# Warm products that read the preamble's constant ones instead of zeros written by VectorE

## The chip, the cores and the metric

One core of one Trainium2 chip. The metric is the device time of one execution in microseconds (us), the median of several. "Span" is the time in the trace from the first to the last instruction; it is about 2.2 us less.

## The reference

Two branches on the same normalised input, added to it: a diagonal state-space layer (S5) and a gated MLP with a spatial product. 2048 rows of 640 columns, bf16 in and out.

```python
x = A_x                                              # (1, 2048, 640)
xn = _layernorm(x, axis=-1)
return x + _A_ref(xn, ...) + _B_ref(xn, ...)         # S5 scan; gelu, layernorm, spatial product, gate
# ... _A_ref, _B_ref and the input setup left out
z = _gelu(einsum('bsd,df->bsf', x, w_in))            # the first matmuls of _B_ref
```

## The kernel before

The kernel describes its work as a graph of operations with assumed durations, plans an order for every engine from them, and derives the semaphore waits from the bytes that each operation reads and writes. A change of an assumed duration can therefore move instructions far away.

The parts that the change touches, and two others:

```python
# loads in the order of the SyncE queue: x tiles and quarters of w_in
FIRST = "x0 x1 x2 h002 h024 h045 x3 h103 x4 h135 x5"
# ...
dve(lambda e: e.memset(zero_m.ap(512), 0.0), [], [zero_m.iv(0, 1024)], 0.25, "zero")
# ... GpSimd builds the identity
act(lambda e: e.activation(zero_m.ap(8, BF16, 1024), zero_m.ap(8), ACT.Gelu_apprx_tanh), [zero_m.iv(0, 1024)],
    [zero_m.iv(1024, 16)], 1.4, "gelu table", bias=9000)      # loads the table early
NW = 7
for n in range(NW):                                           # warms TensorE's clock
    pe(lambda e: e.matmul(ps[:, 7, :], zero_m.ap(128), zero_m.ap(512), start=True, stop=True),
       [zero_m.iv(0, 1024)], [bank(7)], 0.43, "warm")
# ...
DMA_T = tuple(range(7, 16))           # tiles 7 to 15 are transposed by DMA, 0 to 6 by TensorE
def xn_T(i, b=None):
    xn = xc_m[i] if i in EARLY else xns[i]
    if i in DMA_T:
        dma("sp", xnTv[:, :, i * 128:(i + 1) * 128], xn.ap(D), [xn.iv()], xnT_iv(i, i + 1), ..., transpose=True)
        return
    # ... else transposes on TensorE, then a copy out of PSUM by VectorE or ScalarE
```

Behind this come the matmuls of the second half of z (helpers at L701 and L722 in the trace), the scan's inputs, the first half of z, the spatial product and the output. From about 21 us on TensorE works almost without a gap. In the lines, ps is PSUM, the memory that this kernel's matmuls write; PEq is TensorE's sequencer.

Of the kernel before, what the change touches and what calls it, by code (L numbers as in the profile page):

```python
# [7 lines left out]
ACT = mybir.ActivationFunctionType  # L8
# [20 lines left out]
class _Graph:  # L29



    EPS0 = 0.12
    LOOSE, LOOSE_BY = ("cy", "P", "Q", "h7", "fix"), 0.8
    TEPS = 12.0
    DMA_LAT = 2.0
# [68 lines left out]
    def plan(self):  # L105
        ops = self.ops
        keep = dict((o, r) for r, o in self.keep)
        pe = [o for o in ops if o.eng == "pe"]
        nxt = {a: b for a, b in zip(pe, pe[1:])}
        for op in ops:  # L110
            op.start = -1.0
        for op in reversed(ops):
            t = 0.0
            for s in op.succs:
                t = max(t, s.tail)
            own = op.occ + op.lat
            if op.nbytes:
                own += op.nbytes / self.DMA_BW
            t += own
            n = nxt.get(op)  # L120
            if n is not None:
                t = max(t, n.tail + op.occ)
            op.tail = t + op.bias
        free = {}
        dma_free = 0.0
        order = {}
        for op in ops:
            op.npred = len(op.preds)
            op.rdy = 0.0
        avail = {}  # L130
        for op in ops:
            if op.npred == 0:
                avail.setdefault(op.eng, []).append(op)
        pei = 0
        left = len(ops)
        eps = 0.12
        while left:
            best = None
            for eng, lst in avail.items():
                if not lst:  # L140
                    continue
                f = free.get(eng, 0.0)
                if eng == "pe":
                    if pei >= len(pe) or pe[pei].npred:
                        continue
                    cand = pe[pei]
                    st = max(f, cand.rdy)
                else:
                    if eng == "act" and keep:
                        held = {}  # L150
                        for o in lst:
                            t = max(f, o.rdy)
                            if o not in keep:
                                for k, r in keep.items():
                                    if k.start < 0 and t < r + 0.05 and t + o.occ > r + self.KEEP_BY:
                                        t = r + k.occ
                                        break
                            held[o] = t
                        s0 = min(held.values())
                        lst2 = [o for o in lst if held[o] <= s0 + eps]  # L160
                        cand = max(lst2, key=lambda o: o.tail)
                        st = max(f, cand.rdy, s0 if cand not in keep else 0.0)
                        if best is None or st < best[0]:
                            best = (st, cand)
                        continue
                    s0 = min(max(f, o.rdy) for o in lst)
                    cand = max((o for o in lst if max(f, o.rdy) <= s0 + (self.EPS0 if s0 < self.TEPS else eps)), key=lambda o: o.tail)
                    st = max(f, cand.rdy)
                if best is None or st < best[0]:
                    best = (st, cand)  # L170
            st, op = best
            eng = op.eng
            avail[eng].remove(op)
            if eng == "pe":
                pei += 1
            op.start = st
            free[eng] = st + op.occ
            if op.nbytes:
                if op.lat > 2.2:
                    dma_free = max(st + 1.25, dma_free) + op.nbytes / 270e3  # L180
                    free[eng] = st + {163840: 1.28, 819200: 3.6}.get(op.nbytes, 1.45)
                    op.done = dma_free + 2.2
                else:
                    at = max(st + op.occ + 0.9, dma_free)
                    dma_free = at + op.nbytes / (self.DMA_BW0 if at < self.DMA_T0 else self.DMA_BW1 if at < self.DMA_T1 else self.DMA_BW)
                    op.done = dma_free + op.lat - 0.9
            else:
                op.done = st + op.occ + op.lat
            order.setdefault(eng, []).append(op)
            left -= 1  # L190
            for s in op.succs:
                s.npred -= 1
                at = op.start + op.occ if eng == "pe" == s.eng else op.done
                if eng != s.eng and s.eng in ("act", "dve") and s.name.startswith(self.LOOSE):
                    at += self.LOOSE_BY
                if at > s.rdy:
                    s.rdy = at
                if s.npred == 0:
                    avail.setdefault(s.eng, []).append(s)
        self.order = order  # L200
        self.end = max(o.done for o in ops)
        return order
# [38 lines left out]
D = 640  # L241
# [9 lines left out]
def bass_parallel_sum__ssm_conv_s5__mixer_gmlp__prompt_kernel(  # L251
# [17 lines left out]
    with _cl.ExitStack() as _stack, nc.Block() as block:  # L269
# [236 lines left out]
        def load_dskip(after):  # L506
# [6 lines left out]
        dma("act", dk_m.ap(128)[0:16, :], B_w_in[0:640:40, FH:FH + 128], [], [dk_m.iv()], 4096, "touch", bias=9500)  # L513


        dve(lambda e: e.memset(zero_m.ap(512), 0.0), [], [zero_m.iv(0, 1024)], 0.25, "zero")
        pool(lambda e: e.memset(ident_m.ap(128), 0.0), [], [ident_m.iv()], 0.25, "id0")
        pool(lambda e: e.affine_select(out=ident_m.ap(128), in_=ident_m.ap(128), compare_op=ALU.not_equal,
                                       fill=1.0, base=0, pattern=[[-1, 128]], channel_multiplier=1),
# [2 lines left out]
        C("e", 40)  # L522
        pool(lambda e: e.memset(C("half"), -0.5), [], [Civ("half")], 0.2, "mhalf")
        pool(lambda e: e.memset(C("e"), math.e), [], [Civ("e")], 0.2, "e")
        act(lambda e: e.activation(zero_m.ap(8, BF16, 1024), zero_m.ap(8), ACT.Gelu_apprx_tanh), [zero_m.iv(0, 1024)],
            [zero_m.iv(1024, 16)], 1.4, "gelu table", bias=9000)
        NW = 7
        for n in range(NW):
            pe(lambda e: e.matmul(ps[:, 7, :], zero_m.ap(128), zero_m.ap(512), start=True, stop=True),
               [zero_m.iv(0, 1024)], [bank(7)], 0.43, "warm")  # L530

        pslot = [0]

# [21 lines left out]
        ACT_Z2 = (8, 12)  # L555
        NHALF = 4
        SINS = 20
        XT_ACT = (6,)
        BT_AT, BT_DEP = 10, 11
        LASTN = 480  # L560
# [53 lines left out]
        def ln_x(i):  # L614
            xm = xs[i]
            x = xm.ap(D)
            mean, rstd = mrv[:, i, 0:1], mrv[:, i, 1:2]
            mi, ri = mr_m.iv(i * 8, 4), mr_m.iv(i * 8 + 4, 4)
            if i in ACT_LN:
                sq = xn_m[i]  # L620
                act(lambda e: e.activation(sq.ap(D), x, ACT.Copy, scale=1.0 / D, accum_out=mean),
                    [xm.iv()], [sq.iv(), mi], ca(D, acc=1), "lnsum%d" % i)
                act(lambda e: e.activation(sq.ap(D), x, ACT.Square, scale=D ** -0.5, accum_out=stv[:, i, 1:2]),
                    [xm.iv()], [sq.iv(), siv(i, 1, 2)], ca(D, acc=1), "lnsq%d" % i)
                dve(lambda e: e.scalar_tensor_tensor(stv[:, i, 13:14], mean, mean, stv[:, i, 1:2],
                                                     op0=ALU.mult, op1=ALU.subtract, reverse1=True),
                    [siv(i, 1, 2), mi], [siv(i, 13, 14)], 0.07, "lnv%d" % i)
            else:

                held = xnT_iv(2, 3) if i == 3 else [xns[i - 1].iv()] if i in HELD else []  # L630
                dve(lambda e: e.bn_stats(stv[:, i, 0:6], x[:, 0:320]), [xm.iv()] + held, [siv(i, 0, 6)], 0.41, "bn%da" % i)
                dve(lambda e: e.bn_stats(stv[:, i, 6:12], x[:, 320:640]), [xm.iv()] + held, [siv(i, 6, 12)], 0.41, "bn%db" % i)
                dve(lambda e: e.bn_aggr(stv[:, i, 12:14], stv[:, i, 0:12]), [siv(i, 0, 12)], [siv(i, 12, 14)], 0.13,  # L633
                    "bna%d" % i)
            (dve if i in LNE_DVE else pool)(
                lambda e: e.tensor_scalar(stv[:, i, 14:15], stv[:, i, 13:14], 1e-5, None, op0=ALU.add),
                [siv(i, 13, 14)], [siv(i, 14, 15)], 0.07 if i in LNE_DVE else 0.22, "lne%d" % i)
            pool(lambda e: e.tensor_tensor(rstd, stv[:, i, 14:15], C("half")[:, 0:1], ALU.pow),
                 [siv(i, 14, 15), Civ("half")], [ri], 0.55, "rstd%d" % i)
            xn = xn_m[i]  # L640
            xns[i] = xn
            mu = mean if i in ACT_LN else stv[:, i, 12:13]
            dve(lambda e: e.tensor_scalar(xn.ap(D), x, mu, rstd, op0=ALU.subtract, op1=ALU.mult),  # L643
                [xm.iv(), ri, mi if i in ACT_LN else siv(i, 12, 13)], [xn.iv()], cd(D, 4) + 2 * PTR, "xn%d" % i)

        def xn_T(i, b=None):
            xn = xc_m[i] if i in EARLY else xns[i]
# [892 lines left out]
```

## Time and profile before

| | before |
|---|---|
| median, lowest and highest of the first three executions | 261.84, 261.57, 261.86 us |
| span of the profiled execution | 259.4 us |
| TensorE busy | 255.2 us, 98% |
| VectorE busy | 244.3 us, 94% |
| first warm product, first transpose, first real matmul | 1.19, 4.32, 6.08 us |

In a line of the timeline the two first numbers are start and duration in us; what stands in brackets is the idle time of the engine before it and what ended that. In a list of waits the numbers are total us, times, longest. In the chain of waits they are start and duration of each piece.

### The profile page before, as it was taken

To read this page: it belongs to the slowest core of one execution; us is meant where nothing else is said; L and a number is where in the kernel's file an instruction comes from. 1 tells how busy PE (TensorE), PEld (TensorE's weight loads), DVE (VectorE), ACT (ScalarE), POOL (GpSimd) and SP (SyncE) were. 2 spreads that over 40 slices of the span, in tenths; PEclk is the share of its full clock that TensorE was granted. 3 is DMA by queue.
4 is the path that set the end of the run, shared out by engine and by line. 5 is a ranking of instruction groups with operands and counts; after the bars stand their busy time and mean duration, and the time that the engine had idled before them with its cause. 6 is when DMAs were issued, how large, how long until landed. Compare 5 with 4: busy or idle time off the path is not lost.

```text
span 259.4 us, 4334 instructions
## 1 busy us (share of the span) xinstructions
PE 255.2 (98%) x1496; PEld 152.4 (59%) x1500; DVE 244.3 (94%) x567; ACT 179.8 (69%) x323; POOL 26.3 (10%) x50
## 2 busy tenths in 40 slices
PE   7999999999999999999999999999999999999996
PEld 3554554444446777755555555555567777777774
DVE  4899999799999999999999999999999999999943
ACT  6899999799986545442333496873979987895110
POOL 3567065112000000000000000000000000000000
PEclk9999999999999999999999999999999999999999
DMA  6947699999506893399998969991242565457611
GB/s 199 312 121 114 130 175 215 216 299 238 73 1 126 202 207 136 111 316 182 246 217 182 248 159 196 225 209 52 56 133 73 141 172 132 103 140 217 161 63 54
DMA packets 90324, 42.49 MB, mean 164 GB/s; under 512 B 73054, under 2 KB 90302, under 8 KB 90302
## 3 DMA queue, kind: packets, MB, share of 16 engines
q1 hardware_dynamic: 89982, 42.09, 67.2%
q8 instruction: 12, 0.20, 0.3%
q10 hardware_dynamic: 320, 0.12, 0.2%
q14 instruction: 10, 0.08, 0.1%
HBM read 12.28 MB, written 12.45 MB: 95 GB/s over the span
## 4 chain that ended last, share of the span: by engine, by line
PE 95%; DMA 3%; SPq 0%; DVE 0%; issue 0%
PE ps L1116 32%; PE ps L1264 23%; PE ps L701 18%; PE ps L795 17%; PE ps L722 3%; DMA arena<-arena 2%; PE ps L1271 2%; DMA arena<-in_B_w_in_dram 2%; SPq L409 0%; PE ps L659 0%; DVE arena L675 0%; DVE arena L643 0%; DVE arena L1329 0%; DVE arena L633 0%
## 5 line engine op out<-in xcount | busy, mean ns | idle before, releaser
L1116 PE MATMUL ps<-arena 128*128 128x432 bf16 x448 | 81.9, 346 | 0.0
L1116 PEld LDWEIGHTS ps<-arena 128*128 128x128 bf16 x448 | 43.8, 98 | 37.9
L1264 PE MATMUL ps<-arena 128*128 128x320 bf16 (+2 forms) x456 | 64.5, 296 | 0.0
L1264 PEld LDWEIGHTS ps<-arena 128*128 128x128 bf16 x456 | 44.2, 98 | 17.1
L701 PE MATMUL ps<-arena 128*128 128x432 bf16 x280 | 51.9, 346 | 0.2 <-DMA arena<-arena 0.2
L901 ACT ACTIVATE arena<-arena 128x512 bf16<-128x512 bf16 x70 | 46.2, 714 | 1.3 <-DVE arena L905 1.3
L701 PEld LDWEIGHTS ps<-arena 128*128 128x128 bf16 x280 | 34.6, 124 | 16.5 <-DMA arena<-arena 0.6
L795 PE MATMUL ps<-arena 128*128 128x512 bf16 x196 | 43.0, 379 | 0.2
L1129 ACT ACTIVATE arena<-ps,arena 128x432 f32<-128x432 f32 (+1 forms) x32 | 19.8, 620 | 24.9 <-PE ps L1116 23.7
L795 PEld LDWEIGHTS ps<-arena 128*128 128x128 bf16 x200 | 19.6, 98 | 23.5
L824 DVE SCALAR_TENSOR_TENSOR arena<-arena 128x512 f32<-128x512 bf16 x35 | 25.7, 743 | 0.0
L800 ACT CAST arena<-ps 128x512 bf16<-128x512 f32 x40 | 22.1, 602 | 3.7 <-PE ps L795 3.7
L905 DVE TENSOR_TENSOR arena<-arena 128x1024 bf16<-128x1024 bf16 (+1 forms) x42 | 24.3, 593 | 0.0
L779 ACT ACTIVATE arena<-ps 128x864 bf16<-128x864 f32 x16 | 14.3, 891 | 13.9 <-PE ps L701 10.6
L1293 ACT COPY ps<-ps 128x320 f32<-128x320 f32 x24 | 9.9, 411 | 19.8 <-PE ps L1264 19.5
L1285 DVE TENSOR_TENSOR arena<-ps,arena 128x320 bf16<-128x320 f32 (+1 forms) x40 | 18.0, 482 | 5.3 <-PE ps L1271 3.6
L846 DVE TENSOR_TENSOR arena<-arena 128x512 f32<-128x512 f32 (+2 forms) x40 | 21.3, 548 | 0.0
L1071 DVE TENSOR_TENSOR arena<-arena 128x1024 bf16<-128x1024 bf16 x32 | 21.1, 682 | 0.1
L829 DVE SCALAR_TENSOR_TENSOR arena<-arena 128x256 bf16<-128x256 bf16 (+1 forms) x35 | 16.6, 475 | 0.0
L826 DVE SCALAR_TENSOR_TENSOR arena<-arena 128x256 bf16<-128x256 bf16 (+1 forms) x35 | 16.5, 474 | 0.0
L1231 DVE TENSOR_TENSOR arena<-arena 128x640 bf16<-128x640 bf16 x32 | 14.6, 482 | 0.0
L715 ACT ACTIVATE arena<-arena 128x864 bf16<-128x864 bf16 x12 | 11.1, 922 | 0.0
(118 smaller groups left out, 255.8 us busy)
## 6 DMA issues: line engine op xcount, KB each, us to landing
g_scratch<-arena SPq DMA_DIRECT2D x16, 224.0 KB, 2.7
z_scratch<-arena SPq DMA_DIRECT2D x16, 216.0 KB, 2.4
arena<-z_scratch SPq DMA_DIRECT2D x8, 432.0 KB, 4.2
arena<-in_A_x_dram SPq DMA_DIRECT2D x16, 160.0 KB, 3.6
base_scratch<-arena SPq DMA_DIRECT2D x16, 160.0 KB, 2.2
arena<-base_scratch SPq DMA_DIRECT2D x16, 160.0 KB, 3.0
out_dram<-arena SPq DMA_DIRECT2D x15, 160.0 KB, 2.7
arena<-in_B_w_in_dram SPq DMA_DIRECT2D x8, 216.0 KB, 4.2
```

The source lines that it names most:

```text
L701: r = e.matmul(ps[:, b + h, 0:FG], lhs(k), winv[:, k, hcol * FH + h * FG:hcol * FH + (h + 1) * FG], start=(k == 0), stop=(k == ND - 1))
L795: r = e.matmul(ps[:, b, :], btv[:, ri, k, q * 128:(q + 1) * 128], xnTv[:, k, tq * 512:(tq + 1) * 512], start=(k == 0), stop=(k == ND - 1))
L800: act(lambda e: e.copy(o[:, ri, tq], ps[:, b, :].rearrange("p (m j) -> p j m", j=8)), [bank(b)], [l_m.iv((q * 8 + j) * 1024 + ri * 512 + t ...
L824: dve(lambda e: e.scalar_tensor_tensor(tv, prev, lr, cur, op0=ALU.mult, op1=ALU.add), pr + [l_iv(q, j)] + cr, [t.iv()], cd(512) + PTR, nm ...
L846: tt = lambda o, a, b, op: (lambda e: e.tensor_tensor(o, a, b, op))
L901: act(lambda e, pv=pv, hv=hv, lo=lo, sc=sc: e.activation(pv, hv[:, lo:lo + 2, 1:257], ACT.Identity, scale=sc), [h.iv(), Civ(cn)], [m.iv((q ...
L905: dve(lambda e, mv=mv, lq=lq: e.tensor_tensor(lq, lq, mv, ALU.add), li + [m.iv(0, 1024 * n)], li, cd(512 * n, 2), "fix%s%d%d" % (nm, q0, j))
L1071: dve(lambda e: e.tensor_tensor(o.ap(1024), x.ap(1024), y.ap(1024), op), [x.iv(), y.iv()] + S_HELD.get(j, []), [o.iv()], cd(1024, 2), "%s_ ...
L1116: r = e.matmul(ps[:, bk, 0:FG], lv_[:, k, :], rv[k], start=(first and k == 0), stop=(k == 7), skip_group_check=True)
L1129: act(lambda e: e.activation(o, pb(bk), ACT.Identity, bias=bias), [bank(bk)] + bi, [dst], ca(FG, psum=True, ptr=1), name)
L1264: r = e.matmul(ps[:, bk, c0:c1], lf(q), rf(q)[:, c0:c1], start=(first and q == 0), stop=(q == 7), skip_group_check=True)
L1285: dve(lambda e: e.tensor_tensor(o[0][:, c0:c1], ps[:, bk, c0:c1], y[0][:, c0:c1], ALU.add), [bank(bk), y[1]], [o[1]], cd(c1 - c0), "%s_%d" ...
```

## The change

Its intent: the warm products need some operand, no matter which. The preamble of every program already writes constants, a bf16 one per partition among them. If the products read that with a step of zero, VectorE's memset and the wait for it go; the products start earlier, and there is room for an eighth.

```diff
-        dve(lambda e: e.memset(zero_m.ap(512), 0.0), [], [zero_m.iv(0, 1024)], 0.25, "zero")
+        ones = lambda n: nc.const_aps.tensor(1.0, (128, n), BF16)
...
-        act(lambda e: e.activation(zero_m.ap(8, BF16, 1024), zero_m.ap(8), ACT.Gelu_apprx_tanh), [zero_m.iv(0, 1024)],
-            [zero_m.iv(1024, 16)], 1.4, "gelu table", bias=9000)
-        NW = 7
+        act(lambda e: e.activation(zero_m.ap(8), ones(8), ACT.Gelu_apprx_tanh), [], [zero_m.iv(0, 16)], 1.4, "gelu table",
+            bias=9000)
+        NW = 8
         for n in range(NW):
-            pe(lambda e: e.matmul(ps[:, 7, :], zero_m.ap(128), zero_m.ap(512), start=True, stop=True),
-               [zero_m.iv(0, 1024)], [bank(7)], 0.43, "warm")
+            pe(lambda e: e.matmul(ps[:, 7, :], ones(128), ones(512), start=True, stop=True), [], [bank(7)], 0.427, "warm")
... (an empty table of additions to priorities, and a bias of 0.0: without effect)
```

## The prediction

> **What bounds the kernel now.** I read the page's busy table first, then the chain of work that ended last, then the waits of TensorE, and only then the first 22 us in order of time, because the change touches nothing later.
>
> Busy table and clock row of the page:
>
> ```profile
> span 259.4 us, 4334 instructions
> ...
> PE 255.2 (98%) x1496; PEld 152.4 (59%) x1500; DVE 244.3 (94%) x567; ACT 179.8 (69%) x323; POOL 26.3 (10%) x50
> ...
> PEclk9999999999999999999999999999999999999999
> ```
>
> TensorE works for 255.2 of 259.4 us. Those that are left, about 4.2 us, are all that a change without effect on the matmuls themselves could win. The granted clock is full in the row of 40 slices; as shown below, that row does not show the slow first microseconds.
>
> Waits of TensorE in the whole span, and then the chain of waits in its first 20 us:
>
> ```profile
> PE ps L529 <- DVE arena L516: 1.2, 1, 1.2
> PE ps L722 <- DMA arena<-in_B_w_in_dram: 0.3, 1, 0.3
> PE ps L701 <- DMA arena<-arena: 0.2, 1, 0.2
> ```
>
> ```profile
> 2.12 3.91 DMA arena<-in_B_w_in_dram
> 6.03 0.05 issue
> 6.08 1.44 PE ps L722 x6
> ...
> 15.35 0.29 PE ps L659 x5
> 15.64 0.02 issue
> 15.67 0.49 DVE arena L675
> 16.16 0.36 DVE arena L643
> 16.51 0.03 DVE arena L633
> 16.54 4.44 DMA arena<-arena
> ```
>
> TensorE waits three times only. The first wait, 1.2 us, is the one that the change aims at: the warm products (L529) wait for VectorE's zeros (L516). But the chain that sets the end does not go through it. It goes from the issues on the SyncE queue into the load of the weights w_in, which lands at 6.03, and the first real matmul (L722) starts at 6.08. From there TensorE has only 0.2 us of wait left. So the start of the kernel is bound by a transfer whose issues begin at 0.74, and what TensorE does ahead of 6.08 is worth nothing by itself.
>
> The first microseconds in order of time:
>
> ```profile
> 0.86 0.27 DVE L516 MEMSET arena<- 128x256 uint32 x1 [0.86 <-PEq L1525]
> 1.18 1.28 ACT L525 ACT_TABLE_LOAD   x1 [1.18 <-PEq L1525]
> 1.19 3.17 PE L529 MATMUL ps<-arena 128*128 128x512 bf16 x7 [1.19 <-DVE arena L516]
> ...
> 2.48 0.21 ACT L525 ACTIVATE arena<-arena 128x8 bf16<-128x8 bf16 x1
> 3.01 0.74 ACT L572 ACTIVATE arena<-arena 128x640 bf16<-128x640 bf16 x1 [0.32 <-DMA arena<-in_A_x_dram]
> 3.01 0.49 DVE L583 BATCH_NORM_STATS2 arena<-arena 128x6 f32<-128x320 bf16 x1 [1.88 <-DMA arena<-in_A_x_dram]
> ...
> 4.32 0.45 PEld L659 LDWEIGHTS ps<-arena 128*128 128x128 bf16 x5 [0.87 <-DVE arena L577]
> ```
>
> The reader should see that VectorE idles 1.88 us after the memset until x0 lands, that ScalarE idles 0.32 us after its table, and that the first transposes at 4.32 wait for VectorE's centred x0 (L577), not for the warm products.
>
> **What the Trainium skill says.** First, "TensorE: Matmul & The Clock Gate", section "Part 1: The HAM clock gate": the array starts at half rate and goes to full rate after about 3.4 us of activity; the activity window is free-running, so the moment varies from run to run; back-to-back matmuls of 512 columns start 426.7 ns apart cold. The trace agrees with the cold spacing: the seven warm products start from 1.19 to 3.72, six gaps of 0.422 us. It agrees with a release of the clock too, in this query for L722 between 6.5 and 6.6 us:
>
> ```profile
> L722 PE MATMUL ps<-arena x2: 377/453/529, 6.1 to 6.4; 128*128 128x432 bf16 x2
> ```
>
> The first L722 matmul took 529 ns, the second 377, all later ones 346. The first two start 0.36 us apart; later ones 0.184 (20 in 3.68 us). So the clock was released at about 6.4 us, and one real matmul ran cold, a loss of 0.36 - 0.18 = 0.18 us.
>
> Second, "VectorE: DVE Perf Modes", section "Zero memsets can be issued as uint32": one cycle per element whatever the type, and zeros of bf16 go as half as many words. The memset of 512 bf16 is indeed 128x256 uint32 and took 272 ns.
>
> Third, "ScalarE: Activation LUTs", section "What ACT_TABLE_LOAD costs": 1283 ns, as in this trace (1.28), plus a drain of 1380 ns; after this first load no such drain shows, the activation starts at 2.48, 0.02 after the load's end.
>
> **The change part by part.**
> 1. The memset goes: 0.27 us of VectorE at 0.86, in front of an idle stretch of 1.88 us. Worth 0 on the path; VectorE's next work waits for x0 at 3.01 as before.
> 2. The warm products lose their wait. They read the preamble's ones, which the program already wrote before (a memset of 128x1 bf16 at 0.30 by GpSimd, behind the barrier that all engines pass at 0.73 to 0.86). I expect the first product at 0.76 to 0.9, say 0.83 (an estimate from when the other engines start), 0.36 earlier than 1.19. The ones are read with a step of zero; I expect the same 0.422 to 0.427 us each[...]. No run has shown this yet.
> 3. One product more. The slots of the eight take 2.53 + 2 x 0.427 = 3.38 us, so from 0.83 they end at 4.21, against 1.19 + 2.53 + 0.427 = 4.15 before. The transposes are ready at about 4.3, so they start at 4.32 again, with some 0.1 us to spare. Cost 0; if the first product started after 0.93 the transposes would slip by hundredths, which the 0.3 us wait for w_in absorbs in part.
> 4. The table load loses its wait, too. Its start at 1.18 is also just after ScalarE's issue of the small touching load (0.74, 0.41 long, so until 1.15). So the table moves by at most 0.03 us, ahead of 0.32 us of idle time. Worth 0.
> 5. The rest of the diff is inert: the table of additions to priorities is empty and the new bias is 0.0. As to the instruction order, which the kernel plans itself, the warm block is planned to end at 8 x 0.427 = 3.42 us where it ended at 0.38 + 7 x 0.43 = 3.39; the first transposes need x0, its mean and its centring, planned well after both. So I expect the same order on every engine from the first transpose on.
> 6. The clock. Busy time begins 0.36 us earlier and is without a gap for 3.4 instead of 3.0 us. If that brings the release in front of 6.08, the one cold real matmul becomes a warm one: -0.18 us. If the release came before 6.08 anyhow in the timed runs, the gain is 0.
>
> Sum on the path: 0 from the waits, 0 to -0.18 from the clock. Not all of the 0.18 need arrive: at 21.02 TensorE waits 0.15 us for transposes moved by DMA, and these start only after VectorE's L675 and L643, and VectorE is busy for 5.88 of the 6 us from 14 to 20. I put the expectation at -0.1 us: 261.84 - 0.1 = 261.7.
>
> **Rivals.**
> A: The whole advance reaches the end, -0.36 us or even the 1.2 us of the wait (261.5 to 260.6). For it: the wait for L516 is TensorE's longest, and TensorE is 98% busy. Against it: the real matmuls start at 6.08 because w_in lands at 6.03, with its own chain from 0.74. I give it 3%.
> B: The window falls badly. The release is not tied to the start of the kernel, so a run with a later release would have cold real matmuls. An upper estimate from the skill's window of 3.4 us: real matmuls cold from 6.08 for another 3.4 us would lose half of it, 1.7 us, 263.5. For it: in the trace before, the release came only after the real work had begun, so it was not early. Against: before had a shorter block of warm products and three runs within 0.29 us of each other (261.57 to 261.86), so such runs are not common; more warm time makes them rarer, not more common. 5%.
> C: The ones cost something that the zeros did not, by their reading (step zero) or by the activity that the clock looks at. If a product took 0.1 us longer, the block would end at 5.0 instead of 4.2 and delay the transposes by 0.7 us, of which a few tenths might show: 262.1. Nothing in this profile speaks for it, and the clock row is full over all the real matmuls. 4%.
> D: Nothing at all happens, 261.84 within the scatter. This is nearly my main theory, with the release of the clock in the same place.
>
> **Range and chances.** Centre 261.7. The three runs of before scatter by 0.3 us, another session or chip may shift all by as much again (I allow 0.4 each way), and the clock's phase gives -0.2 to some +0.3. So 261.2 to 262.2 holds 8 in 10. Two per cent is 5.2 us. A gain of that size would need more than all 4.2 us in which TensorE is not busy; a loss of that size is three times the upper estimate of B. Faster 1%, same 98%, slower 1%.
>
> **What would show it right or wrong.** In the profile of the changed kernel: no wait of the warm products on VectorE, their first start at 0.76 to 0.9 and eight of them some 0.42 apart; the first transposes at 4.3; the first real matmul at 6.0 to 6.1, still after w_in's landing; its duration near 346 ns if the clock was released before, 529 if not; the same count of VectorE instructions less one and of matmuls plus one; the table load at about 1.15. Wrong would be a first real matmul earlier than 5.9 (A), several real matmuls of 529 ns (B), products spaced over 0.45 us (C), or a different order of instructions after the first transposes, which would open gaps of TensorE that this working does not know.

## The result and the profile after

A ratio here is the mean time of one kernel's fast runs over that of the other's of the same rounds, so it is not quite the ratio of the medians.

| | before | after |
|---|---|---|
| median of 6 executions | 261.77 us | 261.35 us |
| lowest and highest | 261.31, 261.95 | 261.21, 261.94 |
| ratio, 95% interval | | 0.999 (0.9978 to 1.0003) |
| span of the profiled execution | 259.4 us | 259.0 us |

The time is the same. The two profiled executions differ by 0.37 us in span, and it is tempting to give that to the change, since the first real matmul came 0.42 us earlier. (The profiled execution of the changed kernel, 261.21 us, was also the fastest of its six.) The experiments were made to see whether that is so.

First the order of instructions, with the source lines of the two kernels brought into step: on all five engines it is the same but for the edit. (The first trace of before lacks the records of four later matmuls, so it counts 1496 where before_again counts 1500 and the changed kernel 1501.)

```
PE   -L530 Matmult ps<-arena 128x512 x7      +L530 Matmult ps<-const-bfloat16-1.0 128x512 x8
DVE  -L517 Memset arena 128x256
ACT  -L526 Activation arena<-arena 128x8     +L526 Activation arena<-const-bfloat16-1.0 128x8
POOL the same        SP the same
```

The first microseconds of the changed kernel, from its timeline (its lines stand one further down than before, L530 for L529, L723 for L722):

```profile
0.77 3.16 PE L530 MATMUL ps<-const-bfloat16-1.0 128*128 128x512 bf16 x8 [0.77 <-PEq L1526]
...
1.18 1.28 ACT L526 ACT_TABLE_LOAD   x1 [1.18 <-PEq L1526]
...
3.07 0.49 DVE L584 BATCH_NORM_STATS2 arena<-arena 128x6 f32<-128x320 bf16 x1 [3.07 <-DMA arena<-in_A_x_dram]
...
4.37 0.45 PE L660 MATMUL ps<-arena 128*128 128x128 bf16 x5 [0.43 <-DVE arena L578]
...
5.66 1.27 PE L723 MATMUL ps<-arena 128*128 128x432 bf16 x6
```

The products start at 0.77, behind the preamble's barrier. VectorE does nothing until x0 lands, so the memset had cost it nothing. The table load stays at 1.18. The transposes start at 4.37, not earlier than the 4.32 of before; TensorE stood idle for 0.43 us ahead of them in this trace. The first real matmul comes at 5.66.

The query for the warm products in both kernels, before and after:

```profile
L529 PE MATMUL ps<-arena x7: 606/634/634, 1.2 to 3.7; 128*128 128x512 bf16 x7
```

```profile
L530 PE MATMUL ps<-const-bfloat16-1.0 x8: 381/631/631, 0.8 to 3.6; 128*128 128x512 bf16 x8
```

These are durations in ns, least, median and greatest. Ones are neither slower nor faster than zeros (631 against 634). One of the eight took 381: the clock was released while the block was still running. The trace's record of the clock has that moment at 3.39 us here and at 6.46 us in the profile of before.

Now the end of the early stage. The chain of waits of the changed kernel in its first 22 us, the last pieces:

```profile
14.30 0.73 PE ps L702 x4
15.03 0.29 PE ps L660 x5
15.32 0.02 issue
15.35 0.49 DVE arena L676
15.84 0.35 DVE arena L644
16.19 0.03 DVE arena L634
16.22 4.39 DMA arena<-arena
20.61 0.05 issue
20.66 1.45 PE ps L702 x7
```

The end goes through the same four links as before: the transposes of tile 5 on TensorE (L660), their copy (L676), the normalisation of tile 7 (L644), its transpose by DMA, and the matmul that waits for it. Before, that matmul started at 21.02; after, at 20.66. From it to the end of the span both traces have the same length: 259.42 - 21.02 = 238.40 and 259.05 - 20.66 = 238.39 us. So the 0.37 us between the spans is all there at 21 us, and the question is what moves that one matmul. Of the 0.37 us, 0.32 stand already at the transposes of tile 5 (15.35 before, 15.03 after), at their copy and at the issue (16.54, 16.22); 0.05 are flight (4.44, 4.39). So in this pair the later start of before, behind its late w_in, did come through most of the way. TensorE's idle time just before it is short, 0.15 us in before and 0.11 in after: TensorE's own work arrives there almost at the same moment as the transpose.

### The profile page after: what moved, and what is told of

Read it like the earlier page. It is cut to its first block, busy times and chain, and to the rows that moved or that the text cites. A ratio compares the mean times of both kernels' runs of the same rounds, so it can differ in the third digit from the quotient of the medians.

```text
span 259.0 us, 4339 instructions
## 1 busy us (share of the span) xinstructions
PE 254.9 (98%) x1501; PEld 152.1 (59%) x1501; DVE 243.6 (94%) x566; ACT 179.8 (69%) x323; POOL 26.5 (10%) x50
## 4 chain that ended last, share of the span: by engine, by line
PE 92%; DMA 3%; SPq 1%; DVE 1%; POOL 0%; issue 0%
PE ps L1117 32%; PE ps L1265 24%; PE ps L702 18%; PE ps L796 17%; PE ps L1272 2%; DMA arena<-arena 2%; DMA arena<-in_A_x_dram 2%; SPq L410 1%; PE ps L723 1%; DVE arena L676 0%; DVE arena L644 0%; POOL arena L639 0%; PE ps L660 0%; DVE arena L632 0%; DVE arena L633 0%
```

## The experiments

Theory 1: the removed wait is not on the path; what differs from execution to execution is the landing of the first loads, the moment of the clock's release and the flight of the first transpose by DMA, and these made the difference between the two profiles. Theory 2: the earlier start of TensorE reaches the end. Theory 3: the change makes the first loads land sooner (x2 landed at 5.37 us before and at 4.83 after, the first part of w_in at 6.03 and 5.62). Eleven kernels ran, in three calls; the kernels of one call share the chip and the runs of the kernel before.

What the traces say of each profiled execution (times in us from the start of the span; "after 20.6" is the first matmul behind TensorE's wait for the transpose by DMA, "none" where TensorE did not wait there):

| kernel | first product | clock released | w_in lands | first real matmul | after 20.6 | span |
|---|---|---|---|---|---|---|
| before | 1.19 | 6.46 | 6.03 | 6.08 | 21.02 | 259.42 |
| after | 0.77 | 3.39 | 5.62 | 5.66 | 20.66 | 259.05 |
| after_again | 0.77 | 4.44 | 5.52 | 5.57 | 20.93 | 259.31 |
| ones7 | 0.77 | 5.71 | 5.56 | 5.75 | 21.28 | 259.66 |
| ones8_wait | 2.74 | 5.50 | 5.36 | 6.84 | none | 259.70 |
| no_warm | none | 9.61 | 5.58 | 5.74 | 22.64 | 261.02 |
| before_again | 1.19 | 5.69 | 5.48 | 5.73 | 20.80 | 259.50 |
| ones8_wait_dve | 1.19 | 5.51 | 5.45 | 5.97 | 20.80 | 259.19 |
| warm16 | 0.77 | 4.85 | 5.73 | 7.34 | none | 260.17 |
| copy_first | 0.77 | 3.51 | 5.43 | 5.48 | 20.65 | 259.03 |
| after_third | 0.77 | 3.96 | 5.44 | 5.49 | 21.23 | 259.61 |
| xn7_first | 0.77 | 6.64 | 5.38 | 5.75 | none | 259.05 |
| both_first | 0.77 | 3.45 | 5.54 | 5.58 | none | 258.74 |

And the times:

| kernel | median (lowest to highest) | before, same call | ratio (95% interval) |
|---|---|---|---|
| after_again | 261.57 (261.14 to 263.60) | 261.58 | 1.0014 (0.9990 to 1.0038) |
| ones7 | 261.72 (261.22 to 261.92) | 261.58 | 1.0004 (0.9992 to 1.0016) |
| ones8_wait | 262.51 (261.87 to 262.95) | 261.58 | 1.0036 (1.0024 to 1.0048) |
| no_warm | 263.20 (262.46 to 263.53) | 261.58 | 1.0060 (1.0047 to 1.0074) |
| before_again | 261.73 (261.42 to 262.22) | 261.73 | 0.9997 (0.9971 to 1.0023) |
| ones8_wait_dve | 261.52 (261.01 to 261.94) | 261.73 | 0.9989 (0.9963 to 1.0015) |
| warm16 | 262.58 (262.00 to 263.32) | 261.73 | 1.0033 (1.0003 to 1.0063) |
| copy_first | 262.02 (261.28 to 262.36) | 261.73 | 1.0005 (0.9978 to 1.0031) |
| after_third | 261.82 (261.17 to 262.07) | 261.70 | 0.9998 (0.9973 to 1.0024) |
| xn7_first | 261.32 (260.76 to 261.65) | 261.70 | 0.9980 (0.9955 to 1.0005) |
| both_first | 261.19 (260.96 to 261.68) | 261.70 | 0.9981 (0.9953 to 1.0008) |

### after_again, after_third and before_again: the same kernels again

No edit.

> The changed kernel once more, unaltered. Theory 1 (scatter of the first loads and of the clock's release, not the removed wait, made the difference between the two profiles): single times from 261.2 to 262.0 us, overlapping those of the kernel before; the first real matmul starts anywhere from 5.6 to 6.1 us, and the moment when the clock is released differs from the 3.9 us of the first profile. Theory 2 (the removed wait reaches the end): first real matmul again at 5.66 within 0.1, and a time 0.36 us or more below the kernel before in every round. Theory 3 (the change makes the loads of x and w_in land sooner): first real matmul at 5.6 to 5.7 here and at 6.0 to 6.1 in every kernel that keeps the memset.

> The changed kernel a third time, for the mean. Theory 1: median between 261.3 and 261.8, ratio 0.998 to 1.001 to the kernel before; and the rule that all looks without a longer delay have kept so far holds again: span = start of the first matmul after TensorE's wait for the transposes by DMA (at 20.65 to 21.28) + 238.4 us within 0.05, whatever the warm products did. Theory 2: 0.36 us below the kernel before.

> The kernel before, unaltered, against itself: what a ratio of two equal kernels looks like here, and a second look at its first loads. Theory 1 (the late x2 and w_in of the first profile were scatter): x2 lands at 4.6 to 4.9 and the first half of w_in at 5.3 to 5.7, as in every other kernel looked at so far, and the clock is released at some other moment than 6.46; ratio 1.000 within 0.001. Theory 3 (something in the kernel before delays the loads): w_in lands at 6.0 again.

The 0.42 us between the first two medians did not come back: the changed kernel had 261.57 beside 261.58 and 261.82 beside 261.70. Over all executions of the two kernels, the first result included, and without three single ones near 263.6 (one of the changed kernel, two of the kernel before; none of them is among the traces read here, so their cause stays open), the means are 261.60 us (17 executions) and 261.63 us (43). By their scatter of 0.3 us the difference is -0.03 us with a 95% interval of about 0.18 us each way, so it cannot be told from none. (With the three executions both means are 261.71.) Theory 2's 0.36 us is refuted.

Theory 3 is refuted as well: the unaltered kernel before had w_in at 5.48 in its second trace, and in the twelve traces other than the first of before it landed at 5.36 to 5.73, with the memset or without. The 6.03 of the first trace of before was the late outlier. The expectation for after_third that every such span is 238.4 us longer than the start of the matmul at 20.6 to 21.3 held there (259.61 - 21.23 = 238.38). It does not hold for before_again: 259.50 - 20.80 = 238.70, with a pause of TensorE at 196.16 us, where two matmuls start 0.44 us apart, that the other traces do not have; what it waited for was not settled. The median of after_third, 261.82, lies 0.02 us over the expected range.

### ones7: seven products, no wait

```diff
-        NW = 8
+        NW = 7
```

> The changed kernel with seven warm products instead of eight. They end 0.43 us earlier and the first transposes still wait for the centred x0 at about 4.35. Theory 1: same time as the changed kernel within 0.2 us; the release of the clock may come one window later in some executions, which costs at most some tenths of a us. Theory 2: as after_again, the eighth product being without effect. Theory 3: first real matmul at 5.6 to 5.7.

The first transposes at 4.38 again. The release came at 5.71. If the clock's windows of 3.41 us (see the last section) end at the releases, the window before ended at 2.30 and had held too little. The time is that of the changed kernel within 0.2 us. The eighth product shows no gain in time.

### ones8_wait and ones8_wait_dve: the wait put back

```diff
+        dve(lambda e: e.memset(zero_m.ap(512), 0.0), [], [zero_m.iv(0, 1024)], 0.25, "zero")
-    pe(lambda e: e.matmul(ps[:, 7, :], ones(128), ones(512), start=True, stop=True), [], [bank(7)], 0.427, "warm")
+    pe(lambda e: e.matmul(ps[:, 7, :], ones(128), ones(512), start=True, stop=True), [zero_m.iv(0, 1024)], [bank(7)], 0.427, "warm")
     # ones8_wait_dve only: the table's activation writes zero_m.iv(1024, 16), not zero_m.iv(0, 16)
```

> Ones and eight products, but VectorE's memset is kept and the products wait for it, so they start at 1.19 again and their slots end at about 4.58. Theory 1: the first transposes slip from 4.35 to about 4.6, the first real matmul still waits for w_in or for the first copies and starts between 5.7 and 6.1; time between the kernel before and the changed one, 261.2 to 262.0. Theory 2 (the removed wait matters): 261.8 or more, 0.4 slower than the changed kernel. Theory 3: w_in lands late, first real matmul at 6.0 to 6.1.

ones8_wait did not do what it was made for. The table's activation writes the first bytes of the same buffer, so the graph made the products wait for ScalarE:

```profile
2.74 3.25 PE L531 MATMUL ps<-const-bfloat16-1.0 128*128 128x512 bf16 x8 [2.74 <-ACT arena L527]
5.83 0.72 PE L661 MATMUL ps<-arena 128*128 128x128 bf16 x10
6.84 1.27 PE L724 MATMUL ps<-arena 128*128 128x432 bf16 x6 [0.29 <-ACT arena L665]
```

Its expected times were missed, but it is of use. With the products 1.97 us later than in the changed kernel, the transposes are pushed from 4.3 to 5.83 and the time grows by 0.93 us at the median. That is what a warm block costs that stands in the way of real work.

> What ones8_wait was meant to be: eight products of ones that wait for VectorE's memset alone (in ones8_wait they waited for ScalarE's table as well, since its activation wrote the same bytes). Products from 1.19, slots until about 4.58, first transposes at 4.6 instead of 4.35, first real matmul at 5.6 to 5.8. Theory 1: within 0.2 us of the kernel before, ratio 0.999 to 1.001. Theory 2 (what TensorE does first reaches the end one for one): 0.25 to 0.4 us slower than the changed kernel, ratio 1.001 to 1.0015.

With the intended wait the products start at 1.19 and the transposes at 4.57, 0.19 to 0.26 us later than in the changed kernel. The time was 261.52 beside 261.73 of the kernel before. The removed wait of 0.42 us is worth nothing that could be measured. The profiled execution makes the point most plainly: its first real matmul came late (5.97; only the first trace of before and the two kernels whose products hold up the transposes have a later one), and its span (259.19) is 0.42 us shorter than that of after_third, whose first real matmul came at 5.49.

### no_warm and warm16: none, and twice as many

```diff
-        NW = 8
+        NW = 0       # no_warm
+        NW = 16      # warm16; assumed duration halved, so that the planned order stays
```

> The changed kernel without any warm product. Theory 1: the loads and the first real matmul at the same moments (5.6 to 6.1), but the clock is released only [...]at 8 to 10 us: 8 to 20 real matmuls of 432 columns start 0.36 apart instead of 0.18, which costs 1.5 to 3.5 us, less what the wait for the later x loads would have taken anyway (about 0.4): 262.7 to 264.7. Theory 2 would see the first work of TensorE, now the transposes at 4.35, as the thing that counts, with the same large loss; the two are told apart by the other runs. If the warm block were worth nothing the time would stay at 261.4.

```profile
4.37 1.43 PE L660 MATMUL ps<-arena 128*128 128x128 bf16 x10 [4.37 <-DVE arena L578]
5.74 2.32 PE L723 MATMUL ps<-arena 128*128 128x432 bf16 x6
```

The first six real matmuls take 2.32 us from the start of the first to the end of the sixth, where the changed kernel has 1.27. The release came at 9.61, and the query for L723 between 5.7 and 9.5 us has ten matmuls of 421 to 568 ns. TensorE still starts at 4.37 and 5.74, as in the others, so the loss is put down to the clock. The time is 1.62 us longer than that of the kernel before: the block is worth 1.6 us, and before already had that.

> Sixteen warm products instead of eight, same order of everything else. They run cold until the release (3.0 to 6.4 us), then at 0.216 us: the block ends between 5.4 and 7.0, and the transposes start then instead of at 4.35. ones8_wait moved them to 5.83 and cost 0.9 us. Theory 1 (what is worth something is only what delays the transposes past the landing of w_in, or the clock past it): first real matmul at 6.4 to 7.8, all of them warm, +0.5 to +1.7 us on the kernel before. If a longer warm block could help by the clock alone, the time would be 261.2 or less.

The block ended at 6.2 (after the release its products start 0.217 to 0.221 us apart), the first real matmul came at 7.34 and ran at full clock, and the time rose by 0.85 us. More warming than fits before the transposes only pushes the work back.

### copy_first, xn7_first and both_first: the order on VectorE

By theory 1 a gain at the start can be lost again in the waits at 12 us and at 20.7 us. These three change VectorE's order alone, after the plan is made:

```diff
+        x, y = by["dve", "xnT3"], by["dve", "xn4"]     # copy_first: the copy of tile 3 before the normalisation of tile 4
+        x, y = by["dve", "xn7"], by["dve", "xnT5"]     # xn7_first: the normalisation of tile 7 before the copy of tile 5
+        x.start, x.done = y.start - 1e-4, y.start + 0.5
+        g.order["dve"].sort(key=lambda o: o.start)
```

> The changed kernel with one swap in VectorE's order: the copy of the fourth transposed tile goes before the normalisation of x4, for which VectorE stands 0.25 to 0.29 us waiting for GpSimd while TensorE at 12.0 to 12.4 waits for that copy. Theory 1b (a gain at the start is lost again at 12 us, at this wait): no wait of TensorE at 12 us, everything after it 0.2 to 0.4 us earlier, time 0.2 to 0.4 us below the changed kernel, 261.2 at the median, ratio 0.998 to 0.9995. Rival: the next bound, the transposes by DMA that TensorE waits for at 20.7 to 21.3, does not move, and the time stays at 261.5.

TensorE's pause at 12 us is gone, but another opens at 14.10, where it waits for VectorE and two matmuls start 0.46 us apart. The copy of tile 5 then runs at 15.32 (15.35 in the changed kernel), the matmul that waits for the transpose starts at 20.65 (20.66), and the span is 259.03 (259.05). The rival was right, by a longer way than it was written: VectorE's next step took the gain back two microseconds later, and the transpose did not move. This trace is of the fastest of the six executions (261.28); their median, 262.02, is above both expectations, 0.29 us over the kernel before with an interval that holds 1. Why the others were slower is open.

> The changed kernel with one other swap in VectorE's order: the normalisation of x7, which the first transpose by DMA waits for, goes before the copy of the sixth tile (ready at 15.3, runs at 15.75 in the changed kernel). Theory 1c (the end is set by the landing of that first transpose at 20.6 to 21.2, and neither by the warm products nor by the loads ahead of it): its issue at 15.8 to 15.9 instead of 16.2 to 16.6, its landing 0.3 to 0.4 us earlier, TensorE's wait at 20.7 to 21.3 gone, span and time 0.15 to 0.4 us below the changed kernel of the same call. Rival: the copy that is put off makes TensorE wait at 16 to 17 us instead, and the time stays.

> Both swaps in VectorE's order (copy_first and xn7_first). Theory 1c: without the wait at 12 us and with x7 normalised first, TensorE runs without a wait from the first real matmul to the last in some looks; time 0.3 to 0.6 us below the changed kernel, ratio to the kernel before 0.998 to 0.999. Rival: the time is that of xn7_first within 0.1.

The waits of TensorE in after_third, and after them those in xn7_first, of the same call:

```profile
PE ps L530 <- PEq L1526: 0.8, 1, 0.8
PE ps L702 <- DMA arena<-arena: 0.5, 1, 0.5
PE ps L660 <- DVE arena L578: 0.4, 2, 0.3
PE ps L702 <- DVE arena L637: 0.3, 1, 0.3
```

```profile
PE ps L530 <- PEq L1531: 0.8, 1, 0.8
```

The last links of the chain of waits in after_third, and the lines of the timeline of xn7_first for the same three, the copy (L676), the normalisation (L644, two of them in one line) and the issue of the transposes:

```profile
15.57 0.49 DVE arena L676
16.06 0.36 DVE arena L644
16.41 0.03 DVE arena L634
16.44 4.74 DMA arena<-arena
21.18 0.05 issue
21.23 1.82 PE ps L702 x9
```

```profile
15.06 0.95 DVE L644 TENSOR_SCALAR arena<-arena 128x640 bf16<-128x640 bf16 x2
...
15.92 0.48 DVE L676 COPY arena<-ps 128x640 bf16<-128x640 bf16 x1
...
16.04 6.51 SPq L408 DMA_TRANSPOSE arena<-arena  x4
```

In after_third the chain comes to this copy from VectorE's own earlier work, without a pause from 13.89 on, and not from TensorE's transposes of tile 5 as in after: there the order on VectorE alone set the issue. In xn7_first the first transpose by DMA is issued at 16.04 (0.15 us later than was expected) instead of 16.44, lands at 20.62 instead of 21.18, and TensorE has no wait left but the first. This execution had the latest release of all warm kernels (6.64, the first three real matmuls cold) and still ended at 259.05. both_first had an early release and ended at 258.74, the shortest of all traces. By the means of the same call, xn7_first has 261.29, both_first 261.25 and after_third 261.76 us: 0.5 us less than the changed kernel, with one swap of order as with both. That fits the rival written for both_first: the swap of the copies adds nothing that can be seen. Against the kernel before the intervals still touch 1 (0.9955 to 1.0005 and 0.9953 to 1.0008), so a gain of 0.2% is likely and not proven; the change in the waits is seen, in one trace of each.

## Why the prediction was right

The time of 261.35 us lies in the range, "same" was given 98%, and the mean over three calls (261.60) is near the 261.7 predicted. By its own steps:

1. *The memset is worth nothing.* Right: VectorE idles from the start until 3.07.
2. *First product at 0.76 to 0.9, spacing 0.42 to 0.427.* Right: 0.77; and in after_again, cold throughout, eight starts from 0.77 to 3.71, 0.42 apart.
3. *The transposes do not move.* Right: 4.31 to 4.38 in the three traces of the changed kernel, 4.32 and 4.36 in the two of before.
4. *The table load does not move.* Right: 1.18.
5. *The order stays.* Right on all five engines, as far as the records go.
6. *The clock: 0 to -0.18 us.* The earlier release is seen in most traces, its worth in time cannot be. Before, the release came at 6.46 and 5.69; in the changed kernel at 3.39, 4.44 and 3.96. Of the six traces with eight products from 0.77 on, five have it at 3.39 to 4.44, and xn7_first, with the same start, at 6.64. So in these traces an earlier start goes with an earlier release and does not guarantee it. The -0.1 us of the estimate is smaller than 17 executions against 43 can tell (-0.03, 0.18 each way); that the median of 261.35 and the mean of 261.60 fall so near to 261.7 says nothing for this term, and is in part luck.

One reading in the prediction was wrong: that the real matmuls start at 6.08 because w_in lands at 6.03, taken as fixed. That landing was an outlier; in the twelve other traces it lies between 5.36 and 5.73. "The first real matmul at 6.0 to 6.1" was therefore missed (5.66), and it is 5.48 to 5.75 in all the other kernels that hold back nothing. Nor does the landing alone bind it. It starts 0.05 us after the landing in the five traces in which the clock was released before the transposes' end (after, after_again, after_third, copy_first, both_first). In the four in which all ten transposes ran cold and w_in came in time (before_again, ones7, no_warm, xn7_first) TensorE is still at the transposes: it starts at 5.73 to 5.75, 0.16 to 0.37 us after the landing, without a wait. So the clock moves this start too, a term that step 6 lacks; it does not reach the end either. By the prediction's own test for rival A ("a first real matmul earlier than 5.9") one trace would have spoken for A; the repeats showed that this test was badly chosen, since the kernel before has 5.73 too.

The other point was right and too timid: that "not all of the 0.18 need arrive", because of the wait at 21.02. This wait is the last one that TensorE has. In eight of the nine traces that have it, those of no_warm and of the first trace of before among them, the span is the start of that matmul plus 238.38 to 238.40 us, while the first real matmul lies anywhere from 5.48 to 6.08 and does not rank them. That distance says only that no later wait differs; that the landing holds the matmul back is told by TensorE's idle time before it (0.11 to 0.49 us in eight of the nine, under 0.06 in after_again) and by xn7_first, where the wait is gone. Its own scatter, 20.65 to 21.28 in the kernels with a warm block, comes from the issue of the transpose (16.17 to 16.61) and from its flight, 4.27 to 4.77 us.

Of the rivals, A is refuted by ones8_wait_dve and the repeats. B's late release was met once, in xn7_first, with three cold matmuls; whether it cost time cannot be told from one trace (its span is 0.31 us longer than that of both_first, which had an early release and one swap more). C is refuted by the durations, 631 against 634 ns; its other argument, that the clock row is full, was none, since that row is full over the cold start as well (last section).

## What to carry to other kernels

A wait that is the longest of an engine is worth nothing if the engine's next real work waits for something else; look for the last wait that this engine still has, here 0.2 us at 21 us, and ask what releases that one. Before giving a few tenths of a microsecond between two traces to a change, run both kernels once more: here the landing of one load differed by 0.55 us between two traces of one and the same kernel. A block that warms the clock is worth what the cold matmuls would cost (1.6 us here) and must end before real work is ready.

## What the Trainium skill lacked or had wrong

- "TensorE: Matmul & The Clock Gate", section "Part 1: The HAM clock gate": the window agrees (in the traces full clock lasts 256.000 or 252.586 us before a fall at the end; these differ by 3.414 us and are 75 and 74 windows of 3413 ns). The page asks for a busy window and does not say how busy. If a window ends at the moment of release, the one that ended at 3.39 in the changed kernel held products from 0.77 on, at most 2.62 of 3.41 us (77%), and was enough; in xn7_first one window before the release at 6.64 ends at 3.23 with 2.46 us (72%), and was not. A delay between the window's end and the release, which no run here measures, would lower both figures alike.
- The same page, section "Part 4: PE-mode transpose", says of transposes that full clock does not engage for them, since they do not count as busy in the same way. Once the clock is released they do run faster: in the changed kernel the first transposes start 0.056 us apart and take 219 ns each; cold, in before, they start 0.107 us apart and take 314. Whether they count as busy stays open. In ones7 the window from 2.30 to 5.71 holds products until 3.71 (41% of it) and otherwise only the ten transposes (at their spacing of 0.107 us another 30%), and the clock was released. With windows that end at the releases the products alone would not do, since 72% was not enough in xn7_first; but with the transposes it is 71%, hardly enough either. An estimate from the releases and the starts of the matmuls in all thirteen traces: if the release follows its window's end by less than 0.7 us, they fit one threshold only if the transposes count; with a longer delay they fit it without them.
- "ScalarE: Activation LUTs", section "What ACT_TABLE_LOAD costs": 1283 ns agrees; the drain of 1380 ns is not seen behind this first load (load from 1.18 to 2.46, activation at 2.48).
- No page found for it: the clock row of the profile's page shows full speed over the cold start (9 in every slice in before, though the products took 634 ns and a real matmul 529 for 346). The trace's record of the clock begins only with the release (6.46 there).
- No page found for it: how far loads scatter. The first part of w_in, issued at 2.11 to 2.12 us in every trace, landed between 5.36 and 6.03; the first transpose by DMA took 4.07 to 4.77 us.
